# A fused attention and channel-mix kernel: weights loaded as f32, 64x64 tiles, x mixed from SBUF, and a second, general path

## The chip, the cores and the metric

The kernel runs on one core of one Trainium2 chip. The metric is the device time of one execution in microseconds; lower is better. The kernel before was timed three times: 218.06, 219.32 and 219.44, median 219.32. The profile is of one further execution, with a span of 216.9 us.

The core's engines are TensorE (PE; its weight loads are listed as PEld), VectorE (DVE), ScalarE (ACT), GpSimd (POOL) and SyncE (SP), which here only issues DMAs. Each works through its own queue in order.

## The reference

Two blocks one after the other. The first is a linear attention for 8 batches, 8 heads, 576 positions of 64 numbers each; the second is a channel mix over 512 channels (8 heads of 64), with a hidden width of 1024.

```python
q_s = softmax(q, over the 64 numbers);  k_s = softmax(k, over the 576 positions)
kv = k_s^T v                     # 64 x 64 for each head
x  = q_s kv                      # [8, 576, 512]
x_prev = x shifted by one position, zero at the first
xk = mu_k * x + (1 - mu_k) * x_prev
xr = mu_r * x + (1 - mu_r) * x_prev
k = max(xk @ w_k, 0);  v = (k * k) @ w_v
out = sigmoid(xr @ w_r) * v
```

Inputs and output are f32. The softmaxes subtract the maximum before the exponential in the reference. The kernel before leaves that out; for inputs of ordinary size the quotient is the same.

## The kernel before

Everything that TensorE multiplies is bf16, with f32 sums. A batch `b` goes through attention in two halves `u` of four heads each, and the half is laid out so that two heads stand side by side in 128 columns (`h`), and two such pairs on the two halves of the 128 partitions (`g`). 576 positions are split as 64 partitions times `J` = 9.

- `load` (L174): SP loads q, k and v as f32, a half at a time for batches 0 and 1, a whole batch at a time after that. `load_w` and `load_wv` (L240 to L252): GpSimd issues the loads of the three weight matrices, and the DMA turns them into bf16 on the way. `hold` (L189) makes some of these DMAs wait for a step of another engine, to give them an order.
- `exp` (L272, ACT) takes the exponentials of q and k; `cast_v` (L288, mostly GpSimd) makes v bf16, beside a column of ones; `sum_q` and `scale_q` (L292 to L306, DVE) normalize q.
- `turn_q` and `evict_q` (L308 to L320) transpose q on TensorE for batches 0 and 1; for the others `dma_turn_q` (L322) has a DMA do it.
- `kv` (L328): 18 matmuls with 64 rows, 128 columns of weights and 129 columns of data. Only the two diagonal 64x64 blocks of each result are used; column 128 is the sum of the exponentials. `norm_kv` (L342, DVE) divides and writes the blocks into a block-diagonal matrix whose other blocks were zeroed once.
- For batch 0 (`NM` = 1) `x_mixed` (L368) forms xk and xr directly on TensorE, from k'v matrices that were multiplied by mu and 1 - mu beforehand. For batches 1 to 7 `x` (L394) forms x in PSUM, the tile `xp`, with the first 64 columns holding the shifted start. `shift_x` (L405, ACT) reads `xp` and writes (1 - mu) times the previous position into `ak` or `ar`; `mix_x` (L411, DVE) reads the same `xp` and adds mu times x.
- `up` (L419, four matmuls of 288 columns for half of the positions), `relu` (L427, ACT) and `square` (L434, DVE) form k squared for one 128-wide slice `f` of the hidden width. `gate` and `tanh` (L442 to L452) and `down` and `finish` (L454 to L465) handle 128 rows `m` of a pair of batches; `store` (L467) writes them out in two DMAs. The sigmoid is formed as 1 + tanh of half the argument, with the factor 1/2 in relu.

PSUM has eight banks: `mm`, four single ones for up, gate, down and the early transposes and k'v, and `att`, two of two banks for k'v, x and mixed x.

The order of the work is made by a planner, the class `Plan` (L19). Each step has an engine, or several to choose from, a cost in us, a due time, steps it must follow, and slots of buffers that it needs. `run` (L46) plays the plan through: each free engine takes the ready step with the earliest due time whose slots are free. `emit` (L112) then writes the instructions out in that order, so each engine's queue holds them in that order. While nothing else is ready for TensorE before the first `up`, the plan puts in `warm` matmuls (L264), whose result is not used. The due times come from `sequence` and `spread` (L494 to L524): ups of batch `b` are interleaved with the gates and downs of the batches before and with the attention of batch `b` + 1.

Of the kernel before, what the change touches and what calls it, by code (L numbers as in the profile page):

```python
# [10 lines left out]
ALU = mybir.AluOpType  # L12
# [3 lines left out]
BF16 = mybir.dt.bfloat16  # L16


class Plan:  # L19
# [3 lines left out]

    def __init__(self, slots):
        self.slots, self.steps = dict(slots), []

    def slot(self, kind):
        return {"kind": kind, "users": 0, "taken": False}
# [9 lines left out]
    def link(self, s, after, uses):  # L38
# [7 lines left out]
    def run(self, fill=None):  # L46


        todo = {id(s): len(s["next"]) for s in self.steps}
        prev = {id(s): [] for s in self.steps}  # L50
        for s in self.steps:
            for n in s["next"]:
                prev[id(n)].append(s)
        back = [s for s in self.steps if not s["next"]]
        for s in back:
            for p in prev[id(s)]:
                p["due"] = min(p["due"], s["due"] - max(p["eng"].values()) - p["lat"])
                todo[id(p)] -= 1
                if not todo[id(p)]:
                    back.append(p)  # L60
        busy = {e: 0.0 for e in ("DVE", "ACT", "PE", "POOL", "DMA")}
        ready = [s for s in self.steps if not s["left"]]
        events, t, order = [], 0.0, []
        while True:
            for e in busy:
                if busy[e] > t + 1e-9:
                    continue
                for s in sorted(ready, key=lambda s: (s["due"], s["n"])):
# [3 lines left out]
                    for u in s["uses"]:  # L72
                        if not u["taken"]:
                            want[u["kind"]] = want.get(u["kind"], 0) + 1
                    if any(self.slots[k] < c for k, c in want.items()):
                        continue
                    for u in s["uses"]:
                        if not u["taken"]:
                            u["taken"] = True
                            self.slots[u["kind"]] -= 1  # L80
                    ready.remove(s)
                    break
                else:
                    if (not fill or e != fill[0] or "start" in fill[4]
                            or t < fill[3].get("start", 1e9) + 1.3):
                        continue
                    s = {"eng": {e: fill[1]}, "fn": fill[2], "lat": 0.0, "n": -1, "uses": [],
                         "next": [], "due": 0.0}
# [8 lines left out]
            while events and events[0][0] <= t + 1e-9:  # L97
# [6 lines left out]
                if what:  # L104
                    for u in s["uses"]:
                        u["users"] -= 1
                        if not u["users"]:
                            self.slots[u["kind"]] += 1
# [3 lines left out]
    def emit(self, fill=None):  # L112
        for s in self.run(fill):
# [5 lines left out]
def kernel(  # L119
# [21 lines left out]
    HS = S // 2  # L141

    const = ctx.enter_context(tc.tile_pool(name="const", bufs=1))
    ld = ctx.enter_context(tc.tile_pool(name="ld", bufs=2))
    att = ctx.enter_context(tc.tile_pool(name="att", bufs=2))
    grp = ctx.enter_context(tc.tile_pool(name="grp", bufs=2))
    mp = ctx.enter_context(tc.tile_pool(name="mp", bufs=3))
    op = ctx.enter_context(tc.tile_pool(name="op", bufs=4))
    psum = ctx.enter_context(tc.tile_pool(name="psum", bufs=1, space=bass.MemoryType.PSUM))
    MMB, ATB = 4, 2  # L150
    NM = 1


    ident = const.tile([128, 128], BF16, name="ident")
    identf = const.tile([16, 16], F32, name="identf")
    mus = const.tile([16, 64], F32, name="mus")
    mus2 = const.tile([16, 128], F32, name="mus2")
    half = const.tile([16, 2, 64], F32, name="half")
    mine = const.tile([16, 8], F32, name="mine")
    kvms = [const.tile([128, 2, 4, 128], BF16, name=f"kvm{i}") for i in range(2)]  # L160
# [5 lines left out]
    vbs = [const.tile([128, J, 130], BF16, name=f"vb{i}") for i in range(3)]  # L166
    kvbds = [const.tile([128, 2, 128], BF16, name=f"kvbd{i}") for i in range(2)]
    aks = [const.tile([128, S], BF16, name=f"ak{i}") for i in range(3)]
    ars = [const.tile([128, S], BF16, name=f"ar{i}") for i in range(3)]

    st: dict = {}


    def load(n, b, u, behind=None):  # L174


        src = {"q": q, "k": k, "v": v}[n]
        if u in (0, None):
            st[n, b] = ld.tile([128, 2, 2, J * D], F32, tag=n, name=f"{n}t")
        nu = 2 if u is None else 1  # L180
        d = nc.sync.dma_start(
            out=(st[n, b][:].rearrange("p u h f -> p (u h) f") if u is None
                 else st[n, b][:, u, :, :]),
            in_=bass.AP(tensor=src.tensor, offset=src.offset + (b * H + 4 * (u or 0)) * S * D,
                        ap=[[J * D, 128], [2 * S * D, 2 * nu], [1, J * D]]))
        if behind is not None:
            hold(d, behind)

    def hold(d, behind):  # L189

        tc.add_manual_dep(d.ins, st[behind].ins.name, mybir.DependencyInfo(
            mybir.DependencyClass.Sync, mybir.DependencyReason.DATA), reason="load order")

    def load_mu():
        for i, src in enumerate((moe_mu_k, moe_mu_r)):
            nc.scalar.dma_start(out=mus[8 * i:8 * i + 8, :],
                                in_=bass.AP(tensor=src.tensor, offset=src.offset,
                                            ap=[[64, 8], [1, 64]]))

    def pick():  # L200

        heads = identf[:].rearrange("p (a h g) -> p a h g", h=2, g=2)
        halves = const.tile([16, 2], F32, name="halves")
        nc.vector.reduce_sum(out=halves[:], in_=heads.rearrange("p a h g -> p h a g"), axis=AX.XY)
        nc.vector.tensor_copy(out=half[:], in_=halves[:, :, None].to_broadcast((16, 2, 64)))
        nc.vector.tensor_tensor(out=mine[:].rearrange("p (a g) -> p a g", g=2),
                                in0=heads[:, :, 0, :], in1=heads[:, :, 1, :], op=ALU.add)

    def mask_mu():

        nc.vector.tensor_copy(out=mus2[:].rearrange("p (h e) -> p h e", h=2),
                              in_=mus[:, None, :].to_broadcast((16, 2, 64)))
        st["musb"] = musb = mp.tile([16, 8, 64], F32, tag="th", bufs=5, name="musb")
        nc.vector.tensor_tensor(out=musb[:], in0=mus[:, None, :].to_broadcast((16, 8, 64)),
                                in1=mine[:, :, None].to_broadcast((16, 8, 64)), op=ALU.mult)

    def spread_mu():

        rows = psum.tile([128, 8, 64], F32, tag="mm", bufs=MMB, name="mur")
        nc.tensor.matmul(rows[:], lhsT=half[:].rearrange("p h e -> p (h e)"), rhs=st["musb"][:],  # L220
                         start=True, stop=True)
        cols = psum.tile([128, 512], F32, tag="mm", bufs=MMB, name="muc")
        nc.tensor.matmul(cols[:, 0:16], lhsT=mus2[:], rhs=identf[:], start=True, stop=True)
        st["mur"], st["muc"] = rows, cols

    def keep_mu():

        st["mub"] = mub = grp.tile([128, 4, CT, 64], F32, tag="k2", name="mub")
        minus = dict(scalar1=-1.0, scalar2=1.0, op0=ALU.mult, op1=ALU.add)
# [487 lines left out]
```

## Time and profile before

| | |
|---|---|
| median of three runs | 219.32 us |
| span of the profiled execution | 216.9 us |
| first `up` of batch 0 starts | 23.69 us |
| first `up` of batch 1 starts | 48.54 us |
| last matmul ends, about | 211.2 us |
| bytes read from HBM | 33.56 MB |

A row of the page's list of groups reads: line, engine, operation, output and inputs by the program's names, shapes, count, then busy us and mean ns of one, then the idle time of that engine before such instructions and who ended most of it:

```profile
L422 PE MATMUL up<-xk,wk_bf 128*128 128x288 bf16 x512 | 72.5, 286 | 5.0 <-ACT rel L431 4.3
L413 DVE SCALAR_TENSOR_TENSOR xk<-xp,mu,ak 128x576 bf16<-128x576 f32 x28 | 22.6, 814 | 7.4 <-ACT ak L408 4.8
```

Matmuls are pipelined: one row lasts 286 ns, but four of them in a stream take 0.49 us. A row of the timeline has the start in us, the duration in us (of several merged instructions together, with their count), engine, line and operation, and in brackets the idle time before it and who ended it. A row of the list of waits has who waited for whom, then the total in us, how often, and the longest. The chain of waits follows the work that ended last back to the start, and gives each piece the time until the next piece could go.

### The profile page before, as it was taken

Reading aid. Unit: us, or ns where it says so; the run is one execution under the profiler, and the core shown is the slowest. Engines: PE = TensorE matmul, PEld = TensorE weight load, DVE = VectorE, ACT = ScalarE, POOL = GpSimd, SP = SyncE. Lnnn points to the kernel's source line nnn. Section 1 sums busy time; section 2 is a strip of 40 time slices with the busy share of each in tenths; the row PEclk is TensorE's granted clock in tenths of the full one; section 3 lists DMA queues with packets and bytes.
Section 4 is the critical chain, followed back from the end, with each engine's and each line's share of the span. In section 5 each row is a group of like instructions: output and inputs, shape, how many; then the busy total and the mean of one; then the engine's idle time right before and its main releaser. Section 6 shows DMA issues by size and latency. Waiting matters only on the chain.

```text
span 216.9 us, 3766 instructions
## 1 busy us (share of the span) xinstructions
PE 195.5 (90%) x1407; PEld 113.7 (52%) x1428; DVE 159.7 (74%) x251; ACT 143.7 (66%) x265; POOL 26.4 (12%) x41
## 2 busy tenths in 40 slices
PE   0998989999988999999889996999799999999990
PEld 0454657447734665565445554565455565656440
DVE  4859996799999989988878597879887555324221
ACT  4455886997989679769586767669676667445020
POOL 2402820040050120050040002200000000000000
PEclk9999999999999999999999999999999999999997
DMA  6999999867999989998999796062406222322333
GB/s 224 381 241 368 345 189 362 335 182 211 210 353 311 302 282 313 271 352 276 304 229 365 175 383 128 14 141 48 103 3 151 48 51 48 88 57 51 72 85 87
DMA packets 34977, 44.15 MB, mean 204 GB/s; under 512 B 16016, under 2 KB 17552, under 8 KB 34960
## 3 DMA queue, kind: packets, MB, share of 16 engines
q1 hardware_dynamic: 32656, 41.16, 64.7%
q0 software_dynamic: 2192, 2.62, 7.1%
q8 instruction: 11, 0.18, 0.3%
q10 hardware_dynamic: 112, 0.14, 0.2%
q14 instruction: 6, 0.05, 0.1%
HBM read 33.56 MB, written 9.44 MB: 198 GB/s over the span
## 4 chain that ended last, share of the span: by engine, by line
PE 71%; DVE 16%; ACT 6%; issue 3%; DMA 1%; ACTq 0%; DVEq 0%
PE vp L457 27%; PE up L422 22%; PE rp L445 11%; PE kvp L338 4%; DVE qs L303 3%; ACT ar L408 3%; DVE xk L413 3%; PE warm L269 3%; DVE xr L413 2%; DVE rs L295 2%; PE xp L399 2%; DMA mus<-in_moe_mu_r_dram 1%; ACT rel L431 1%; PE qtp L313 1%; ACT ak L408 1%
## 5 line engine op out<-in xcount | busy, mean ns | idle before, releaser
L422 PE MATMUL up<-xk,wk_bf 128*128 128x288 bf16 x512 | 72.5, 286 | 5.0 <-ACT rel L431 4.3
L457 PE MATMUL vp<-wv_bf,k 128*128 128x512 bf16 x276 | 66.1, 379 | 0.7
L431 ACT ACTIVATE rel<-up 128x288 bf16<-128x288 f32 x128 | 49.8, 420 | 18.0 <-PE up L422 15.9
L422 PEld LDWEIGHTS <-wk_bf 128*128 128x128 bf16 x512 | 48.1, 98 | 23.8 <-issue 6.5
L457 PEld LDWEIGHTS <-k 128*128 128x128 bf16 x288 | 27.6, 98 | 30.6 <-issue 0.8
L463 DVE SCALAR_TENSOR_TENSOR ot<-th,vp 128x512 f32<-128x512 f32 x36 | 24.4, 685 | 24.2 <-PE vp L457 12.3
L445 PE MATMUL rp<-wr_bf,xr 128*128 128x512 bf16 x137 | 35.4, 379 | 1.7 <-ACT rel L431 1.3
L451 ACT ACTIVATE th<-rp 128x512 f32<-128x512 f32 x36 | 21.2, 613 | 18.4 <-PE rp L445 17.9
L286 POOL CAST vb<-vt 128x1152 bf16<-128x1152 f32 x15 | 19.4, 1311 | 102.4 <-DMA vt<-in_v_dram 87.0
L413 DVE SCALAR_TENSOR_TENSOR xk<-xp,mu,ak 128x576 bf16<-128x576 f32 x28 | 22.6, 814 | 7.4 <-ACT ak L408 4.8
L413 DVE SCALAR_TENSOR_TENSOR xr<-xp,mu,ar 128x576 bf16<-128x576 f32 x28 | 22.6, 812 | 7.0 <-ACT ar L408 6.5
L408 ACT ACTIVATE ar<-xp,om 128x575 bf16<-128x575 f32 x28 | 20.7, 746 | 9.8 <-DVE xk L413 9.8
L439 DVE TENSOR_TENSOR k<-rel 128x1152 bf16<-128x1152 bf16 x32 | 24.1, 754 | 2.8 <-ACT rel L431 2.5
L408 ACT ACTIVATE ak<-xp,om 128x575 bf16<-128x575 f32 x28 | 20.6, 746 | 8.3 <-PE xp L401 8.3
L303 DVE TENSOR_TENSOR qs<-eq,rr 128x1152 bf16<-128x1152 bf16 x16 | 24.6, 1538 | 0.2
L295 DVE TENSOR_REDUCE rs<-eq 128x18 f32<-128x1152 bf16 x16 | 21.6, 1349 | 1.0 <-ACT eq L274 0.7
L445 PEld LDWEIGHTS <-xr 128*128 128x128 bf16 x144 | 13.9, 98 | 15.0 <-issue 2.5
L274 ACT ACTIVATE eq<-qt 128x1152 bf16<-128x1152 f32 x16 | 19.0, 1186 | 1.5 <-DMA qt<-in_q_dram 1.5
L274 ACT ACTIVATE ek<-kt 128x1152 bf16<-128x1152 f32 x16 | 19.0, 1192 | 0.9 <-DMA kt<-in_k_dram 0.9
L338 PE MATMUL kvp<-vb,ek 64*128 64x129 bf16 x288 | 11.4, 218 | 0.0
L338 PEld LDWEIGHTS <-ek 64*128 64x128 bf16 x288 | 8.5, 94 | 4.6 <-issue 3.6
L399 PE MATMUL xp<-qT,kvbd 128*128 128x448 bf16 x28 | 9.3, 353 | 0.7 <-DVE xr L413 0.5
(54 smaller groups left out, 93.8 us busy)
## 6 DMA issues: line engine op xcount, KB each, us to landing
out_dram<-ot SPq DMA_DIRECT2D x71, 128.0 KB, 2.5
qt<-in_q_dram SPq DMA_DIRECT2D x6, 1152.0 KB, 6.8
kt<-in_k_dram SPq DMA_DIRECT2D x6, 1152.0 KB, 8.0
vt<-in_v_dram SPq DMA_DIRECT2D x6, 1152.0 KB, 8.1
qt<-in_q_dram SPq DMA_DIRECT2D x4, 576.0 KB, 7.1
kt<-in_k_dram SPq DMA_DIRECT2D x4, 576.0 KB, 7.3
vt<-in_v_dram SPq DMA_DIRECT2D x4, 576.0 KB, 10.6
wk_bf<-in_moe_w_k_dram POOLq DMA_DIRECT2D x4, 256.0 KB, 8.6
```

What stands on the lines that cost most here:

```text
L274: st["exp", n, b, u] = nc.scalar.activation(out=e[:].rearrange("p j (h d) -> p h j d", h=2), in_=st[n, b][:, u, :, :].rearrange("p h (j d) ...
L295: nc.vector.reduce_sum(out=rs[:], in_=eq, axis=AX.X)
L303: ew(eng).tensor_tensor(out=qs[:].rearrange("p j (h d) -> p (j h) d", h=2), in0=eq, in1=st["rr", b, u][:, :, None].to_broadcast((128, 2 * ...
L338: nc.tensor.matmul(ps[g][:, 0:129], lhsT=ek[r, j, :], rhs=vb[r, j, 0:129], start=(j == 0), stop=(j == J - 1))
L408: nc.scalar.activation(out=(aks, ars)[w][(4 * b + ct) % 3][:, 1:], in_=st["xp", b, u, g][:, 1:S], func=ACT.Copy, scale=om[:, c:c + 1])
L413: nc.vector.scalar_tensor_tensor(out=blend(b, ct, w), in0=st["xp", b, u, g][:, 64:], scalar=mu[:, 4 * w + ct:4 * w + ct + 1], in1=(aks, ar ...
L422: nc.tensor.matmul(ps[:, 0:HS], lhsT=wk_bf[:, ct, 128 * f:128 * f + 128], rhs=st["xk", b][:, ct, HS * h:HS * h + HS], start=(ct == 0), sto ...
L431: nc.scalar.activation(out=st["rel", b, f // 2][:, f % 2, HS * h:HS * h + HS], in_=st["up", b, f, h][:, 0:HS], func=ACT.Relu, scale=0.5 ** ...
L439: nc.vector.tensor_tensor(out=st["k2", b // 2][:, 2 * f2:2 * f2 + 2, o:o + S], in0=r[:], in1=r[:], op=ALU.mult)
L445: nc.tensor.matmul(ps[:], lhsT=st["xr", i][:, ct, 128 * m:128 * m + 128], rhs=wr_bf[:, ct, :], start=(ct == 0), stop=(ct == CT - 1))
L457: nc.tensor.matmul(ps[:], lhsT=st["k2", i][:, f, 128 * m:128 * m + 128], rhs=wv_bf[:, f, :], start=(f == 0), stop=(f == FT - 1))
L463: nc.vector.scalar_tensor_tensor(out=ot[:], in0=st["th", i, m][:], scalar=1.0, in1=st["vp", i, m][:], op0=ALU.add, op1=ALU.mult)
```

## The change

The same function is computed, from the same inputs, on the same engines. What differs:

- **Loads.** All loads stand in one SP queue, in the order q, q, k, v, k, v of batch 0; w_k in two pieces; w_r; batch 1; w_v in two pieces, which wait until w_k's buffer has been cast. The weights arrive as f32 in the buffers that later hold `k2` and `xr`, and are cast to bf16 on chip in ten pieces, most of them on GpSimd. Loads of all batches are a half at a time, with three buffers each. `hold` is gone.
- **64x64 tiles.** `kv` multiplies each head by itself: 36 matmuls of 64 rows, 64 columns of weights and 65 columns of data. `x` uses eight matmuls of 64 rows and 64 columns. The block-diagonal matrices and their zeros go; `norm_kv` becomes one reciprocal and one multiplication.
- **x from SBUF.** `evict_x` copies x from PSUM to SBUF (`xs`) on ACT in two parts, `prefix` copies the shifted start on GpSimd, `shift_x` runs on GpSimd or ACT (the planner puts 31 on GpSimd and 17 on ACT), and `mix_x` reads `xs` in place of PSUM.
- **Two batches mixed by TensorE** (`NM` = 2): batches 0 and 1 take the way of `x_mixed`, on 64x64 tiles, with `weigh_kv` on DVE.
- **relu** takes 576 columns at once; `square` may run on ACT.
- **PSUM**: three tiles of two banks (`two`) for up, k'v, x and transposes, and two of one bank (`one`) for gate and down.
- **General path.** The reciprocals of all sums are kept in `inv`. Near the end `watch`, `gather` and `judge` count those within 1e-6 to 1e6; every engine reads the flag, and if one is outside, a second program (`general`) computes everything again with the maxima subtracted. It more than doubles the instructions of the program, and is skipped with these inputs.
- **Planner**: buffers are chosen by the plan, due times start at 16.5 for batch 0's ups and 34.0 for batch 1's, and `warm` matmuls go into the gaps of the finished plan: six stand in TensorE's queue. In that queue three downs of batch 0 stand ahead of the first `up` of batch 1.

The core of the diff:

```diff
-                d = nc.gpsimd.dma_start(
...
-    def load_wv():
-        nc.gpsimd.dma_start(out=wv_bf[:], in_=bass.AP(
-            tensor=moe_w_v.tensor, offset=moe_w_v.offset, ap=[[C, 128], [128 * C, FT], [1, C]]))
...
+    def load_wk(a):
+        nc.sync.dma_start(out=wk_raw()[:, a, :, :], in_=bass.AP(
+            tensor=moe_w_k.tensor, offset=moe_w_k.offset + a * F // 2,
+            ap=[[F, 128], [128 * F, CT], [1, F // 2]]))
...
+    def load_wv(a):
+        nc.sync.dma_start(out=wv_raw()[:, 4 * a:4 * a + 4, :], in_=bass.AP(
+            tensor=moe_w_v.tensor, offset=moe_w_v.offset + 4 * a * 128 * C,
+            ap=[[C, 128], [128 * C, 4], [1, C]]))
+
+    def cast_wk(eng, a, c):
+        copy(eng, wk_bf[:, :, 512 * a + 256 * c:512 * a + 256 * c + 256],
+             wk_raw()[:, a, :, 256 * c:256 * c + 256])
...
+        ps, ek, vb = at("two", "kv", b, u), at("ek", b, u), at("vb", b, u)
         for j in range(J):
             for g in range(2):
-                r = slice(64 * g, 64 * g + 64)
-                nc.tensor.matmul(ps[g][:, 0:129], lhsT=ek[r, j, :], rhs=vb[r, j, 0:129],
-                                 start=(j == 0), stop=(j == J - 1))
-        st["kvp", b, u] = ps if b < 2 else t
...
-        if b < 2:
+                for h in range(2):
+                    r = slice(64 * g, 64 * g + 64)
+                    nc.tensor.matmul(ps[64 * h:64 * h + 64, g, 0:65],
+                                     lhsT=ek[r, j, 64 * h:64 * h + 64], rhs=vb[r, j, h, :],
+                                     start=(j == 0), stop=(j == J - 1))
...
+        rz = inv_k(b, u)
+        nc.vector.reciprocal(out=rz, in_=ps[:, :, 64])
+        nc.vector.tensor_tensor(out=dst[:], in0=ps[:, :, 0:64],
+                                in1=rz[:, :, None].to_broadcast((128, 2, 64)), op=ALU.mult)
+
+    def weigh_kv(b, u, w):
+        nc.vector.tensor_tensor(
+            out=at("kvm", b, u)[:, w, :, :, :].rearrange("p o g e -> p o (g e)"),
+            in0=at("kvn", b, u)[:].rearrange("p g e -> p (g e)")[:, None, :].to_broadcast(
+                (128, 2, 128)),
+            in1=mub(u)[:, w, :, :], op=ALU.mult)
...
+    def x(b, u, c):
+        ps, qT, kvs = at("two", "x", b, u, c), at("qT", b, u), at("kvs", b, u)
+        lo, n = PARTS[c]
+        for g in range(2):
+            for h in range(2):
+                r = slice(64 * h, 64 * h + 64)
+                nc.tensor.matmul(ps[64 * g:64 * g + 64, h, 0:64 * n], lhsT=kvs[r, g, :],
+                                 rhs=qT[r, lo:lo + n, 64 * g:64 * g + 64], start=True, stop=True)
...
+    def evict_x(b, u, c):
+        lo, n = PARTS[c]
+        copy("ACT", at("xs", b, u)[:, :, 64 + 64 * lo:64 + 64 * (lo + n)],
+             at("two", "x", b, u, c)[:, :, 0:64 * n])
+
+    def prefix(b, u):
+        xs = at("xs", b, u)
+        copy("POOL", xs[:, :, 1:64], xs[:, :, S:S + 63])
...
+    def shift_x(eng, b, u, h, w):
+        ct = 2 * u + h
+        o, i, s = at("aw", b, ct, w)[:], at("xs", b, u)[:, h, 0:S], om[:, 4 * w + ct:4 * w + ct + 1]
+        if eng == "ACT":
+            nc.scalar.activation(out=o, in_=i, func=ACT.Copy, scale=s)
         else:
-            nc.vector.reciprocal(out=rz[:], in_=ps[:, :, 128])
-        for h2 in range(2):
...
-    def mix_x(b, u, g, w):
-        ct = 2 * u + g
+            nc.gpsimd.tensor_scalar(out=o, in0=i, scalar1=s, scalar2=1.0, op0=ALU.mult,
+                                    op1=ALU.mult)
+
+    def mix_x(b, u, h, w):
+        ct = 2 * u + h
         nc.vector.scalar_tensor_tensor(
-            out=blend(b, ct, w), in0=st["xp", b, u, g][:, 64:],
-            scalar=mu[:, 4 * w + ct:4 * w + ct + 1],
-            in1=(aks, ars)[w][(4 * b + ct) % 3][:], op0=ALU.mult, op1=ALU.add)
-
-
-    def up(b, f, h):
-        ps = psum.tile([128, 512], F32, tag="mm", bufs=MMB, name="up")
+            out=blend(b, w)[:, ct, :], in0=at("xs", b, u)[:, h, 64:],
+            scalar=mu[:, 4 * w + ct:4 * w + ct + 1], in1=at("aw", b, ct, w)[:], op0=ALU.mult,
+            op1=ALU.add)
+
...
+    def up(b, f):
+        ps, xk = at("two", "up", b, f), at("xk", b)
+        for a in range(2):
+            for ct in range(CT):
+                nc.tensor.matmul(ps[:, a, 0:HS], lhsT=wk_bf[:, ct, 128 * f:128 * f + 128],
+                                 rhs=xk[:, ct, HS * a:HS * a + HS], start=(ct == 0),
+                                 stop=(ct == CT - 1))
...
+    def relu(b, f):
+        nc.scalar.activation(
+            out=at("rel", b, f // 2)[:, f % 2, :].rearrange("p (a c) -> p a c", a=2),
+            in_=at("two", "up", b, f)[:, :, 0:HS], func=ACT.Relu, scale=0.5 ** 0.5)
...
+    def square(eng, b, f2):
+        o, r = S * (b % 2), at("rel", b, f2)
+        dst = at("k2", b // 2)[:, 2 * f2:2 * f2 + 2, o:o + S]
+        if eng == "ACT":
+            nc.scalar.activation(out=dst, in_=r[:], func=ACT.Square)
+        else:
+            nc.vector.tensor_tensor(out=dst, in0=r[:], in1=r[:], op=ALU.mult)
...
-    pl = Plan({"mm": MMB, "att": ATB, "eq": 3, "ek": 3, "qs": 2, "qT": 3, "vb": 3, "xk": 2, "xr": 2,
-               "k2": 2, "th": 5, "rel": 3, "ot": 4, "a0": 3, "a1": 3, "bd0": 1, "bd1": 1, "ldq": 2, "ldk": 2, "ldv": 2})
...
+    def watch():
+        nc.vector.tensor_scalar(out=okay[:], in0=inv[:], scalar1=LOW, scalar2=None, op0=ALU.is_ge)
+        nc.vector.scalar_tensor_tensor(out=okay[:], in0=inv[:], scalar=HIGH, in1=okay[:],
+                                       op0=ALU.is_le, op1=ALU.mult)
+        nc.vector.reduce_sum(out=count[:], in_=okay[:], axis=AX.X)
+
+    def gather():
+        nc.tensor.matmul(at("two", "flag")[0:1, 0, 0:1], lhsT=count[:], rhs=ones[:], start=True,
+                         stop=True)
+
+    def judge():
+        nc.vector.tensor_scalar(out=flag[:], in0=at("two", "flag")[0:1, 0, 0:1],
+                                scalar1=128.0 * NR - 0.5, scalar2=None, op0=ALU.is_lt)
+
+    def read_flag():
+        st["bad"] = nc.values_load(flag[:], min_val=0, max_val=1,
+                                   skip_runtime_bounds_check_because="a comparison gives 0 or 1")
+        tc.mark_branch_hint_location("general")
...
+    queue = [ld("q", 0, 0), ld("q", 0, 1), ld("k", 0, 0), ld("v", 0, 0), ld("k", 0, 1),
+             ld("v", 0, 1)]
+    for a in range(2):
+        queue.append(dma(2.7, 0.0, lambda a=a: load_wk(a), uses=[sl("k2", "w")]))
...
+    for a in range(2):
+        queue.append(dma(2.7, 0.0, lambda a=a: load_wv(a), uses=[sl("k2", "w")],
+                         after=[ev["wk", i] for i in range(4)]))
...
     with tc.manual_schedule():
-        pl.emit(("PE", 0.3, warm, ev["mup"], ev["up", 0, 0, 0]))
+        pl.emit(("PE", 0.6, warm, ev["mup"], ev["up", 0, 0]))
+        slot = Turns()
+        with tc.If(st["bad"] != 0, preferred_fallthrough_block=False, label="general"):
+            general()
```

More of the change, by code (lines that the diff above doesn't have):

```diff
@@ L83, in run @@
                 else:
[L84 to L88, printed above, removed]
+                    continue
                 s["start"], s["on"], s["cost"] = t, e, s["eng"][e]
@@ L161 @@
+    mine = const.tile([8, 4], F32, name="mine")
+    halves = const.tile([8, 2], F32, name="halves")
     mu = const.tile([128, 8], F32, name="mu")
@@ L189, in hold @@
[L189 to L224, printed above, removed]
```

769 lines of the change are left out of this document (408 added, 361 removed).

## The prediction

> **What bounds the kernel now.** I read the busy totals and the chain of waits first, then the timeline of the first 50 us, then the list of who waited for whom, and last the rows of the operations that change.
>
> ```profile
> PE 195.5 (90%) x1407; PEld 113.7 (52%) x1428; DVE 159.7 (74%) x251; ACT 143.7 (66%) x265; POOL 26.4 (12%) x41
> ...
> PE 71%; DVE 16%; ACT 6%; issue 3%; DMA 1%; ACTq 0%; DVEq 0%
> ```
>
> TensorE is the bound, but not throughout. The timeline gives two marks: the first `up` of batch 0, and the first `up` of batch 1. The GpSimd row between them shows when the third batch of v had landed.
>
> ```profile
> 23.69 3.10 PE L422 MATMUL up<-xk,wk_bf 128*128 128x288 bf16 x24
> ...
> 44.38 2.24 POOL L286 CAST vb<-vt 128x1152 bf16<-128x1152 f32 x2 [14.58 <-DMA vt<-in_v_dram]
> ...
> 48.54 0.65 PE L422 MATMUL up<-xk,wk_bf 128*128 128x288 bf16 x4
> 49.13 0.70 PE L338 MATMUL kvp<-vb,ek 64*128 64x129 bf16 x18
> ```
>
> From the chain, an `up` of four matmuls takes 0.49, a gate 0.865, a down 1.73, a k'v 0.63. All ups, gates and downs are 128 x 0.49 + 36 x 0.865 + 36 x 1.73 = 156.1 us. At 48.4 batch 0's ups, four gates and four downs are done (7.8 + 3.5 + 6.9 = 18.2), so 137.9 is left, and 12 k'v and 12 x pairs (x: 0.27 for each g, so 0.54): 12 x 1.17 = 14.0. The last matmul ends at 211.2: 162.8 us for 151.9 of work. Of the 10.9 lost, these waits name 6.3:
>
> ```profile
> ACT ar L408 <- DVE xk L413: 9.8, 12, 1.4
> ...
> PE up L422 <- ACT rel L431: 4.3, 3, 1.4
> ...
> PE rp L445 <- ACT rel L431: 1.3, 5, 0.5
> PE up L422 <- ACT th L451: 0.7, 1, 0.7
> ```
>
> ACT stands still behind a `shift_x` that waits for DVE to finish with the same PSUM tile `xp`; relu queues behind it, its PSUM is not freed, PE stops. The other 4.6 is spread thin and stays in my sum. After the last matmul come tanh, finish, store and its landing, 211.2 to 216.9: 5.7 us.
>
> **The change, part by part.** Sums are against the span, 216.9; the median of the runs, 219.32, lies 2.4 above it, and I add that at the end.
>
> *Loads.* Three batches (3 x 3.54 MB) and the weights (5.24 MB as f32) were read by 44.4, the first 0.59 MB by 4.5: 15.3 MB in 39.9 us, 384 GB/s of reading. The new single queue reads batch 0, w_k, w_r, batch 1, w_v: 12.33 MB, so w_v ends at 4.5 + 11.74 / 0.384 = 35.1. On the way v of batch 0 is in at 12.2, the halves of w_k at 14.9 and 17.6, w_r at 20.4, v of batch 1 at 29.6. GpSimd casts the weights at the rate of L286 (1.15 for 1152, so 1.02 per piece of 1024); w_v's last pieces are ready at about 36.2.
>
> *First ups.* DVE now stands in order: reduce 1.35 and reciprocal 0.27, the mu rows (2.0, from about 8.0), again 1.6, two scalings of 1.36, then norms, weighings and copies of about 0.43 each; the first mixed x can start at about 16.5 and its copies end at 19. GpSimd casts w_k from 14.9 to 20 beside the weighings, which puts 1 us on them: first up at about 20 instead of 23.7. But what follows waits for w_v: in the new order on PE three downs of batch 0 stand ahead of batch 1's first up. So 36.2 + 3 x 1.73 + 1.4 for the mixed x between them = 42.8. There are few warming matmuls left (30 before); the early ones took 0.43 against 0.216 later, while the granted clock reads 1.00, so I add 0.7: batch 1 starts at 43.5, with 7.8 + 3.5 + 5.2 = 16.5 done. Before: 48.4 with 18.2. Gain 4.9 - 1.7 = 3.2, from -4 (the loads run at the 306 GB/s that the first eight slices count as moved: w_v at 42.9) to 6.
>
> *k'v and x on 64x64 tiles.* k'v goes from 18 matmuls of 129 columns to 36 of 65, each with its own weight load. No row has a 64-column tile. Below: 0.63 x 65/129 = 0.32. Above: L338's 35 ns a piece, 1.26, or without overlap of loads still more (a rival). Nearest is the 63-column piece of x, about 30 ns: 36 x 30 = 1.08 one after another, and 0.68 if row halves overlap as in L338 (129 columns serially are 56 ns, measured 35). I take 0.70. x: eight matmuls, 2304 columns, 0.98 serially, 0.61 with that overlap, 0.38 if column halves overlap too; I take 0.50 for 0.54. Twelve of each: 14.4 for 14.0, +0.4, from -6 to +8.
>
> *x mixed from SBUF.* Away go 48 `shift_x` reads of PSUM on ACT (0.746); in come 24 copies (0.64 and 0.59), and the shifts divide: 31 on GpSimd, 17 on ACT. relu goes from two of 0.41 to one of about 0.66; some squares move to ACT. Over the two batches from 109.1 to 157.3 ACT is busy 34.2 and DVE 38.7, 17.1 and 19.3 in a period of 24.1. The new ACT load is within 1 us of the old; DVE loses about 1.9 (mix 0.82 to about 0.75, one square or more of 0.75). The wait of ACT for DVE on `xp` is gone, so the 6.3 can go. What is late next is this:
>
> ```profile
> 24.20 1.20 POOL L286 CAST vb<-vt 128x1152 bf16<-128x1152 f32 x1
> ...
> 24.22 2.40 DVE L303 TENSOR_TENSOR qs<-eq,rr 128x1152 bf16<-128x1152 bf16 x1
> ...
> 72.28 1.36 DVE L303 TENSOR_TENSOR qs<-eq,rr 128x1152 bf16<-128x1152 bf16 x1
> ```
>
> A DVE operation with two SBUF inputs stood still while GpSimd worked: 2.40 for 1.36. Now mix_x has two SBUF inputs as well. Per batch GpSimd is busy 2 x 1.15 + 5.2 shifts x 0.65 (the cast's rate; a dearer one is possible, 1.2) + 2 x 0.25 = 6.2 of 22, DVE has about 12.6 such operations, and each meets it 28% of the time for 0.4: 1.4 us. DVE is at 17.4 + 1.4 = 18.8 of a period that PE alone makes 22: it holds, with bubbles. Two slots for gate and down, three for everything else, take slack away too. I leave 3.0 of the 6.3: gain 3.3, from 6.3 to a loss (rival one).
>
> *General path.* Not entered with these inputs. `watch`, `judge` and the 1x1 matmul run beside the last downs, when DVE is 20% busy: nothing. Every engine loads a register from SBUF before the last two or three tiles and ends with a branch over the other path. No row shows either; below nothing is excluded, as both only add. Nearest is a DMA's landing, 2.5: between 0 (hidden under the last store) and 4; I take 1.5.
>
> Sum: 216.9 - 3.2 + 0.4 - 3.3 + 1.5 = 212.3, and 2.4: **214.7 us**.
>
> **Rivals.**
> [...] If each of the 12.6 waits is a whole shift (0.65) and some a cast, 8 us, DVE needs 25.4 a batch and becomes the bound; it decides from waits of 6.7 (17.4 + 6.7 = 24.1). Six batches x 1.3 = 7.8: 219.3 - 3.2 + 1.5 + 0.4 + 7.8 = 225.8; half way, 223. For: the 2.40. Against: only three of 16 scalings show it (median 1.358).
> [...]
> *Two, slower: weight loads bound the small tiles.* A load row lasts 94 ns; if only the two row halves overlap, k'v is 18 x 94 = 1.7, +1.07 x 12 = 12.8: 227. For: 36 loads replace 18. Against: L338's 18 loads fit in 0.52.
> [...]
> *Three: the loads give nothing.* At 306 GB/s batch 1 starts at 51.3: 222; at 345, 218.
> *Four, faster: all bubbles go and the tiles overlap fourfold:* 214.7 - 3.0 - 3 = 208.5.
>
> **How the numbers follow.** Forecast (211 to 218.5) 0.42, of which 0.1 lies within 1% of 219.3 (about what can be told from no change); four 0.17; one 0.18; two 0.08; three 0.15, of which 0.06 within 1%. Faster 0.32 + 0.17 = 0.49, same 0.16, slower 0.35. The range leaves out two and the worst of one and three above, and the last of four below: 207 to 225.
>
> **What would show it.** Batch 1's first `up` at 43 to 44, w_v's casts just before; k'v near 0.7 in the chain; no wait of ACT for DVE on an x tile; DVE at 18 to 19 a batch, mix_x near 0.75 with some at 1.4; the last matmul near 205. It is wrong if mix_x averages over 1.1, if a k'v takes over 1.2, or if w_v lands after 39.

## The result, and the profile after

| | before | after |
|---|---|---|
| median of 12 runs each, us | 219.22 (218.06 to 220.12) | 217.52 (214.92 to 218.65) |
| ratio after/before | | 0.9898, 95% interval 0.9866 to 0.9929 |
| profiled execution: time, span, us | 219.32, 216.9 | 218.41, 217.0 |

The kernel became 1.0% faster (0.7 to 1.3%); 2.1% was forecast. The ratio leaves out the four of the twelve executions after that lie over 1.5% above the fastest, which is one reason why it is lower than that of the medians, and the profiled execution, 0.9 us above the median, is one of the four. Its span is no shorter than that of before; 1.7 us of it are lost to a low clock behind a stop of TensorE, read below.

The page's busy totals after:

```profile
PE 186.2 (86%) x1799; PEld 106.6 (49%) x1824; DVE 154.8 (71%) x216; ACT 145.8 (67%) x205; POOL 70.6 (33%) x81
```

TensorE is busy for 9.3 us less in the same span. Most of this is no saving: the `warm` matmuls, whose result is not used, fell from 9.5 to 2.9 us. From the first `up` of batch 1 to the last matmul TensorE is busy 153.6 us of 164.5, where it was 154.8 of 162.7. The PE timeline gives the marks: the first `up` of batch 0 at 19.55 (23.69 before), the first of batch 1 at 45.25 (48.54), and a k'v and an x of a later batch (a k'v row lasts 0.75 at 10.78 and 0.48 from 32.30 on, though the granted clock reads 1.00 from 0 to 40).

```profile
19.55 5.15 PE L448 MATMUL two<-xk,wk_bf 128*128 128x288 bf16 x40
...
45.25 1.14 PE L448 MATMUL two<-xk,wk_bf 128*128 128x288 bf16 x8
...
68.51 0.48 PE L364 MATMUL two<-vb,ek 64*64 64x65 bf16 x36
68.92 1.15 PE L448 MATMUL two<-xk,wk_bf 128*128 128x288 bf16 x8
...
72.71 0.44 PE L415 MATMUL two<-qT,kvs 64*64 64x256 bf16 x8
73.08 1.90 PE L477 MATMUL one<-wv_bf,k 128*128 128x512 bf16 x8
```

From its start to the start of the next row a k'v now takes 0.41 us (0.63 before) and an x 0.37 (0.54). TensorE's waits from 45.2 us on (who waited for whom: us in total, times, longest):

```profile
PE two L448 <- DVE xk L438: 4.7, 4, 2.2
PE one L477 <- DVE ot L482: 2.5, 2, 1.7
PE two L415 <- DVE kvs L373: 1.0, 2, 0.6
```

The old waits for relu are gone, and ups now wait for `mix_x` on VectorE, downs for `finish`. The groups of the new mixing (busy us, mean ns of one, idle before):

```profile
L438 DVE SCALAR_TENSOR_TENSOR xk<-xs,mu,aw 128x576 bf16<-128x576 f32 x24 | 28.6, 1229 | 6.9 <-POOL aw L433 6.8
...
L433 POOL TENSOR_SCALAR aw<-xs,om 128x576 bf16<-128x576 f32 x31 | 29.8, 977 | 5.0 <-POOL xs L221 4.8
...
L438 DVE SCALAR_TENSOR_TENSOR xr<-xs,mu,aw 128x576 bf16<-128x576 f32 x24 | 22.2, 955 | 0.0
```

A `mix_x` takes 1.09 us on the mean of its 48. The list by tiles has the shortest, the median and the longest of each (in ns, then first and last start in us):

```profile
L438 DVE SCALAR_TENSOR_TENSOR xk<-xs,mu,aw x24: 806/1293/1704, 52.3 to 178.6; 128x576 bf16<-128x576 f32 x24
L438 DVE SCALAR_TENSOR_TENSOR xr<-xs,mu,aw x24: 803/806/1704, 54.2 to 180.8; 128x576 bf16<-128x576 f32 x24
```

A mix with two SBUF inputs thus took 0.81 when nothing of GpSimd's stood beside it (two in a row 1.53 at 65.89, behind the end of a cast). Most mixes of `xr` did, and only four of them, each beside a cast of v, took 1.70. Of the mixes of `xk`, 22 of 24 were longer than 0.9, 16 of them about 1.29, beside a shift. The timeline in front of batch 2's ups shows how one instance comes about (start, us, engine, what, and the wait ahead of it):

```profile
57.99 1.61 POOL L221 CAST vb<-ldv 128x1152 bf16<-128x1152 f32 x1 [4.35 <-PE two L415]
...
58.51 2.30 DVE L334 TENSOR_TENSOR qs<-eq,inv 128x1152 bf16<-128x1152 bf16 x1
...
59.55 1.41 POOL L221 COPY xs<-xs 128x126 f32<-128x126 f32 x1
...
61.05 2.69 POOL L433 TENSOR_SCALAR aw<-xs,om 128x576 bf16<-128x576 f32 x3
...
61.84 2.51 DVE L438 SCALAR_TENSOR_TENSOR xk<-xs,mu,aw 128x576 bf16<-128x576 f32 x2 [1.03 <-POOL aw L433]
...
63.18 0.28 PE L448 MATMUL two<-xk,wk_bf 128*128 128x288 bf16 x1 [2.19 <-DVE xk L438]
64.40 0.90 PE L448 MATMUL two<-xk,wk_bf 128*128 128x288 bf16 x5 [0.94 <-DVE xk L438]
...
65.95 2.63 PE L477 MATMUL one<-wv_bf,k 128*128 128x512 bf16 x6 [0.22 <-issue]
```

GpSimd's cast of v (1.15 alone) stretches the VectorE scaling from 1.36 to 2.30, the scaling stretches the small prefix copy from 0.29 to 1.41, the shifts start late, and shifts and mixes stretch each other: two mixes in 2.51 us. TensorE stands for 3.1 us, and the six matmuls of a down behind it take 2.63 instead of some 1.4: the granted clock reads 0.73, 0.50 and 0.92 in the three stretches of 2 us from 64 to 70, so 1.7 us are lost.

At the end the last store is issued at 210.48 and the span ends at 217.0, 6.5 us later (4.2 before).

### The profile page after: what moved, and what is told of

Read it like the earlier page. It is cut to its first block, busy times and chain, and to the rows that moved or that the text cites. A ratio compares the mean times of both kernels' runs of the same rounds, so it can differ in the third digit from the quotient of the medians.

```text
span 217.0 us, 4567 instructions
## 1 busy us (share of the span) xinstructions
PE 186.2 (86%) x1799; PEld 106.6 (49%) x1824; DVE 154.8 (71%) x216; ACT 145.8 (67%) x205; POOL 70.6 (33%) x81
## 5 line engine op out<-in xcount | busy, mean ns | idle before, releaser
L448 PE MATMUL two<-xk,wk_bf 128*128 128x288 bf16 x512 | 72.4, 286 | 6.1 <-DVE xk L438 4.7
L477 PE MATMUL one<-wv_bf,k 128*128 128x512 bf16 x274 | 67.7, 385 | 4.3 <-DVE ot L482 3.3
L453 ACT ACTIVATE rel<-two 128x576 bf16<-128x576 f32 x64 | 41.3, 651 | 29.7 <-PE two L448 29.2
L482 DVE SCALAR_TENSOR_TENSOR ot<-th,one 128x512 f32<-128x512 f32 x36 | 24.5, 683 | 30.0 <-PE one L477 20.4
L467 PE MATMUL one<-wr_bf,xr 128*128 128x512 bf16 x133 | 34.8, 379 | 1.1 <-ACT th L472 0.6
L438 DVE SCALAR_TENSOR_TENSOR xk<-xs,mu,aw 128x576 bf16<-128x576 f32 x24 | 28.6, 1229 | 6.9 <-POOL aw L433 6.8
L221 POOL CAST vb<-ldv 128x1152 bf16<-128x1152 f32 (+1 forms) x18 | 24.0, 1340 | 26.8 <-DMA ldv<-in_v_dram 20.6
L433 POOL TENSOR_SCALAR aw<-xs,om 128x576 bf16<-128x576 f32 x31 | 29.8, 977 | 5.0 <-POOL xs L221 4.8
L334 DVE TENSOR_TENSOR qs<-eq,inv 128x1152 bf16<-128x1152 bf16 x16 | 22.6, 1415 | 0.1
L438 DVE SCALAR_TENSOR_TENSOR xr<-xs,mu,aw 128x576 bf16<-128x576 f32 x24 | 22.2, 955 | 0.0
```

The costliest lines, as they stand in the source:

```text
L221: return {"DVE": nc.vector, "POOL": nc.gpsimd}[eng].tensor_copy(out=out, in_=in_)
L334: nc.vector.tensor_tensor(out=at("qs", b, u)[:].rearrange("p j (h d) -> p (j h) d", h=2), in0=at("eq", b, u)[:].rearrange("p j (h d) -> p ...
L433: nc.gpsimd.tensor_scalar(out=o, in0=i, scalar1=s, scalar2=1.0, op0=ALU.mult, op1=ALU.mult)
L438: nc.vector.scalar_tensor_tensor(out=blend(b, w)[:, ct, :], in0=at("xs", b, u)[:, h, 64:], scalar=mu[:, 4 * w + ct:4 * w + ct + 1], in1=at ...
L448: nc.tensor.matmul(ps[:, a, 0:HS], lhsT=wk_bf[:, ct, 128 * f:128 * f + 128], rhs=xk[:, ct, HS * a:HS * a + HS], start=(ct == 0), stop=(ct ...
L453: nc.scalar.activation(out=at("rel", b, f // 2)[:, f % 2, :].rearrange("p (a c) -> p a c", a=2), in_=at("two", "up", b, f)[:, :, 0:HS], fu ...
```

## Experiments

Each kernel is the changed one with the edit shown. A difference to the changed kernel is one between medians; its own executions spread from 214.92 to 218.65, and taken from the ratios to before, the gains below come out up to 1.4 us smaller. Two theories of the stops: P, VectorE operations with two SBUF inputs and GpSimd operations stretch each other; W, the chain copy, prefix, shift, mix through GpSimd is long by itself.

### The general path left out

```diff
-    a = pl.step("DVE", 1.0, d - 6.0, watch, after=[nk, ...
-    ...
-    pl.step("PE", 0.1, d, read_flag, after=[a])
-        with tc.If(st["bad"] != 0, ...): general()
```

> Left out: watch, gather, judge, read_flag, the branch and the second path behind it; all that is computed for these inputs stays. Theory of the end (the branch costs what the span shows behind the last store: 6.5 us after its issue, before 4.2): the stretch from the end of the last matmul to the end of the span falls from 7.3 us to 5 to 5.7, the time by 1.6 to 2.3 us, to about 215.5. Theory that the end is only the landing of the last store: the stretch stays at 7, the time at 217 to 217.5.

214.78 us, ratio to before 0.9827 (0.9783 to 0.9871), 2.7 us less than the changed kernel. Head and last row of its timeline:

```profile
core 0 of [0], span 213.2 us
...
209.63 0.55 ACTq L490 DMA_DIRECT2D out_dram<-ot  x1
```

The span ends 3.6 us after the last store's issue instead of 6.5. The end is a cost of its own. How much time it is worth is less sure: 0.7 us more was gained than the 215.5 expected, and the interval of the ratio just touches the changed kernel's (0.9866 to 0.9929).

### The shifts on GpSimd left out, and the wait for them alone

```diff
+    still = const.tile([128, S], BF16, name="still")        # zeroed once
-            ... in1=at("aw", b, ct, w)[:], op0=ALU.mult,
+            ... in1=still[:], op0=ALU.mult,
-            nc.gpsimd.tensor_scalar(out=o, in0=i, scalar1=s, ...)    # only without the shifts
```

> Left out: the 31 shift_x on GpSimd (the 17 on ScalarE stay); every mix_x reads a bfloat16 tile that was zeroed once, so the token before is missing from the mix. The order of all other instructions is that of the changed kernel. Theory P (VectorE operations with two SBUF inputs and GpSimd operations stretch each other): mix_x falls from a mean of 1.09 us (48 of them) to 0.75 to 0.85, VectorE's busy time by 10 us or more, the 4.7 us of up waiting for mix_x to under 1, the time to 211 to 213. Theory W (not the stretching, but the longer chain copy, prefix, shift, mix in front of the ups): the same time, but mix_x stays near 1.0 because the stretching is not what made it long.

> All shift_x stay on GpSimd and ScalarE, but mix_x reads the zeroed tile: the wait of mix_x for its shift is gone and GpSimd is as busy as before; the token before is missing from the mix. Theory P: mix_x stays near 1.05 us on the mean, the time stays above that of the run without the shifts by 2 us or more (215 to 217). Theory W: as fast as the run without the shifts, within 0.7 us.

208.9 us (0.9565, 0.9525 to 0.9606) without the 31 shifts; 211.22 (0.9672, 0.963 to 0.9713) with the shifts there but nothing waiting for them. The groups, first without, then with the shifts:

```profile
L439 DVE SCALAR_TENSOR_TENSOR xk<-xs,mu,still 128x576 bf16<-128x576 f32 x24 | 21.8, 950 | 4.0 <-ACT xs L221 4.0
```

```profile
L435 POOL TENSOR_SCALAR aw<-xs,om 128x576 bf16<-128x576 f32 x31 | 35.8, 1169 | 5.3 <-ACT xs L221 4.2
...
L440 DVE SCALAR_TENSOR_TENSOR xk<-xs,mu,still 128x576 bf16<-128x576 f32 x24 | 25.9, 1119 | 4.0 <-ACT xs L221 4.0
```

VectorE's busy time falls by 12 us without the shifts (142.8) and by 2 with them unread (152.8). The shifts are worth 8.6 us in all. Neither theory had the second number: 2.3 us stay when nothing waits, more than W allows, and 6.3 go, more than P said. The length of the chain and the stretching are not told apart here: both edits change both.

### mix_x with one SBUF input, still waiting for its shift

```diff
-            ... in0=at("xs", b, u)[:, h, 64:],
+            ... in0=bufs["two"][2][:, 0, None, 448:512].to_broadcast((128, J, 64)),
```

> mix_x takes its first operand from a constant strip of 64 columns in PSUM, repeated nine times, instead of x in SBUF (so x at the token itself is missing from the mix); it still waits for its shift, on GpSimd or ScalarE, and has the same size. It has one SBUF input instead of two. A few matmuls wait for a mix_x that reads the same bank, which can only cost. Theory P (the stretching makes the chain long): mix_x falls to 0.82 us (what it took from PSUM before), the shifts on GpSimd to 0.9 or less, the waits of up for mix_x from 4.7 to under 2 us, time 209 to 212.5. Theory W (GpSimd's steps are long by themselves, whatever VectorE does): shifts stay at 0.98, the waits at 4 us or more, time 215 to 217.

217.57 us (0.9885, 0.9839 to 0.993): no change against the changed kernel, where theory P gave 209 to 212.5, and inconclusive. `mix_x` did fall to 0.81 and the shifts to 0.78, but ups now waited 5.9 us for mixes of `xr`, which only shared a bank with them. In the second form each of the three slots holds the strip, and a mix takes the one that TensorE wrote neither last nor longest ago:

```diff
+            in0=bufs["two"][st["seen"][1]][:, 0, None, 448:512].to_broadcast((128, J, 64)),
```

> As the earlier run with the constant PSUM strip as mix_x's first operand (x at the token itself is missing), but the strip is in each of the three two-bank slots and each mix_x takes the one that TensorE wrote neither last nor longest ago, so that TensorE should rarely have to wait for a mix_x that only shares its bank. Shifts and prefix stay on GpSimd and mix_x waits for them. Theory P (what VectorE and GpSimd do to each other's instructions makes the time): mix_x 0.82, shifts 0.8 or less, waits of up for mix_x under 3 us, time 211 to 214.5. Theory W (the chain through GpSimd costs this even without that): waits of up for mix_x 4 us or more, 216 to 217.5.

210.16 us (0.9597, 0.955 to 0.9644), 7.4 us less than the changed kernel. Its groups, the shortest, median and longest mixes, and TensorE's waits:

```profile
L441 POOL TENSOR_SCALAR aw<-xs,om 128x576 bf16<-128x576 f32 x31 | 24.7, 810 | 4.1 <-POOL xs L227 4.0
...
L446 DVE SCALAR_TENSOR_TENSOR xr<-two,mu,aw 128x576 bf16<-128x576 f32 x24 | 18.8, 810 | 1.7 <-ACT rel L463 1.0 <-PE two L372 0.4 <-POOL vb L227 0.2
L446 DVE SCALAR_TENSOR_TENSOR xk<-two,mu,aw 128x576 bf16<-128x576 f32 x24 | 18.7, 812 | 7.8 <-POOL aw L441 7.0 <-PE two L458 0.5 <-ACT rel L463 0.3
```

```profile
L446 DVE SCALAR_TENSOR_TENSOR xk<-two,mu,aw x24: 805/811/819, 52.1 to 169.8; 128x576 bf16<-128x576 f32 x24
L446 DVE SCALAR_TENSOR_TENSOR xr<-two,mu,aw x24: 804/809/818, 54.7 to 171.9; 128x576 bf16<-128x576 f32 x24
```

```profile
PE two L458 <- DVE xk L446: 1.9, 2, 1.4
```

GpSimd has all its work, every mix waits for its shift as before (7.0 us of VectorE waiting for `aw`), and only the second SBUF input of `mix_x` is gone. This is theory P, at 7.4 us (6.6 from the ratios), better than the range it gave. No mix is longer than 0.82 now, and that is no gain of reading PSUM as such, since an undisturbed one from SBUF took 0.81 too. In the profiled executions some 1.7 us of the gain is the low clock behind the stop: this one has none between its first `up` and its last matmul. Shifts fell with the mixes, from 0.98 to 0.81 on the mean. Why the two stretch each other is shown by no run.

### Shifts, and the prefix, on ScalarE

```diff
-                    p = pl.step({"POOL": 0.7, "ACT": 0.7}, 0, dx + 1.5 + 0.7 * h + 1.4 * w,
+                    p = pl.step({"ACT": 0.77}, 0.77, dx + 1.5 + 0.7 * h + 1.4 * w,
```

> All 48 shift_x on ScalarE, nothing else changed; the plan orders anew. Theory P: mix_x falls to 0.75 to 0.9 us, ScalarE takes on 31 x 0.77 = 24 us (busy about 165 to 170, unless squares go over to VectorE), waits of up for mix_x under 2 us, time 213 to 216. Theory W: a shift is shorter by only 0.2 us of a chain of four steps, and ScalarE is fuller: 217 to 220.

210.2 us (0.9587, 0.9521 to 0.9652), better than P's range. ScalarE is busy 156.3 us, not 165, because eight squares stay with it instead of 15, and mixes take 0.89 on the mean. So nearly all that the kernel with the strip in three slots showed is to be had with the whole computation. The prefix alone on ScalarE, with the 31 shifts left on GpSimd:

```diff
-        copy("POOL", xs[:, :, 1:64], xs[:, :, S:S + 63])
+        copy("ACT", xs[:, :, 1:64], xs[:, :, S:S + 63])
```

> Only prefix (12 copies of 126 columns, 0.3 us when nothing stands in the way) goes from GpSimd to ScalarE; the 31 shifts on GpSimd stay where they are. In the changed kernel's trace the prefix of batch 2 took 1.41 us, behind a cast of v on its own queue and beside a VectorE scaling of 2.30 us. If that one link is what opens the hole of 3.1 us at 61 to 64 us and the slow clock behind it (1.5 us): 214 to 215.5. If the shifts and mixes make it (four of the 5 us between x and the first up are theirs): within 1 us of the changed kernel, 216.5 to 218.

217.6 us (0.9892, 0.9852 to 0.9931): nothing gained. The prefix of batch 2 fell from 1.41 to 0.33, and the time went into the next link, three shifts in 4.37 us, beside a scaling and a square of VectorE:

```profile
59.64 4.37 POOL L433 TENSOR_SCALAR aw<-xs,om 128x576 bf16<-128x576 f32 x3
```

From 45.2 us on, ups waited 0.9 us for `mix_x` instead of 4.7, but downs waited 3.5 us for a tanh (none before) and 3.7 for `finish` (2.5 before): the waits of the ups alone do not say what the stretching costs.

With both on ScalarE:

> All shift_x and prefix on ScalarE; GpSimd only casts v (and, early, weights). Against the run with the shifts alone there (210.2): its prefixes still took 0.55 us on the mean, so where one of them is in a hole 1 us goes: 208.5 to 210. If ScalarE (75% busy there) becomes the bound, 210.5 to 212.

209.8 us (0.9563, 0.9523 to 0.9604), the same as with the shifts alone. A hole of 1.57 and 0.45 us in TensorE's work, at batch 2's first ups, stays.

### Batch 2 mixed by TensorE

```diff
-    NM = 2
+    NM = 3
```

> Batch 2 is mixed by TensorE as well (NM = 3), everything else as in the changed kernel. The hole of 3.1 us that TensorE has at 61 to 64 us, waiting for batch 2's mix_x, and the slow clock behind it (1 to 1.5 us) go; TensorE gets four x_mixed pairs (4 x 0.69) for two x (2 x 0.44), 1.9 us more, and nine transposes twice (1.1 more). Theory P or W alike: -4 + 3 = about -1, 216 to 217.5. If the hole only moves to batch 3: 218 to 220.

214.96 us (0.9817, 0.9765 to 0.9869), 2.6 less, where 216 to 217.5 was expected (the interval overlaps a little with the changed kernel's); TensorE is busy 191.9 instead of 186.2, and the hole at 61 us is gone. Together with shifts and prefix on ScalarE:

> As the run with shifts and prefix on ScalarE, with batch 2 mixed by TensorE too. In the changed kernel this was worth 2.6 us because it went round the hole of batch 2. If moving the shifts has closed that hole already, only TensorE's extra work is left (1.9 us of x_mixed, 1.1 of transposes): 2 to 3 us slower than without it, 211 to 213. If there is still a hole there, the same time within 1 us.

208.81 us (0.9529, 0.9487 to 0.9571), against 209.8 without: 1 us faster. A hole had been left, and for this case the same time within 1 us was expected; the 2 to 3 us slower belonged to the case without one. TensorE is busy 2.8 us longer, and its idle time shrinks by more.

### The end together with the rest

> All shift_x on ScalarE and no watch, branch and second path (as in the two runs that did one of these alone; for these inputs nothing is missing). If the end is a cost of its own, behind everything, the two gains add: 210.2 - 2.3 to 2.7 = 207.5 to 208. If the end's gain came from other instructions being placed differently, less than 1 us is left of it: 209.3 to 210.2.

> As the run with shifts and prefix on ScalarE, and no watch, branch and second path (nothing that these inputs need is missing): the end's 2.0 to 2.7 us less than that run, 206.5 to 208; if the hole in front of batch 2's ups is gone too, the mean granted clock is at 0.995 or above and the spans at 204 to 206.

> Shifts and prefix on ScalarE, batch 2 mixed by TensorE, no watch, branch and second path. 208.8 without the last; the end was worth 1.1 to 2.7 us in three pairs: 206.3 to 207.7.

208.56 (against 210.2), 208.73 (against 209.8) and 207.14 us (0.9444, 0.9428 to 0.9459; against 208.81): the end gives 1.6, 1.1 and 1.7 us here, less than the 2.7 of the first pair and less than two of the three expectations. From the last store's issue to the end of the span the middle pair (209.8 and 208.73) has 5.5 and 3.6 us, 1.9 less. In its two profiled executions the clock took part of this back: both have the same hole, and the ups behind it took 2.73 us in one, with the granted clock at 1.00, and 4.19 in the other, with 0.51 and 0.64 in the 2 us stretches from 64 and 66. First the run with the general path, then without:

```profile
61.79 0.28 PE L448 MATMUL two<-xk,wk_bf 128*128 128x288 bf16 x1 [1.57 <-DVE xk L438]
62.52 2.73 PE L448 MATMUL two<-xk,wk_bf 128*128 128x288 bf16 x21 [0.45 <-DVE xk L438]
```

```profile
62.22 0.28 PE L448 MATMUL two<-xk,wk_bf 128*128 128x288 bf16 x1 [1.56 <-DVE xk L438]
62.95 4.19 PE L448 MATMUL two<-xk,wk_bf 128*128 128x288 bf16 x21 [0.45 <-DVE xk L438]
```

The kernel of 207.14 us beats both; it has no path for inputs out of range, as the kernel before had none. With that path, 208.81 is the fastest measured.

### PSUM slots, the tiles, and the order of the loads

```diff
-    bufs["two"] = [... for i in range(3)]
-    bufs["one"] = [... for i in range(2)]
+    bufs["two"] = [... for i in range(2)]
+    bufs["one"] = [... for i in range(4)]
```

> PSUM split anew: two slots of two banks and four of one bank, instead of three and two. The stops of downs for finish (2.5 us of waits, and 0.13 us in each of the last tiles) go, at most 3.3 us. If the third slot of two banks is what keeps ups going while relu, copies and k'v hold theirs, more than this comes back as ups that wait for relu: 219 to 224. If two are enough, 214 to 216.

228.03 us (1.0376, 1.0311 to 1.0442), above the 219 to 224 expected. Downs no longer wait for `finish`, and ups wait 6.3 us for `mix_x` and 4.2 for `norm_kv` (for relu, as was expected, 1.4); the third slot of two banks is worth more than the stops of downs.

```diff
-        for j in range(J):
+        for j in [*range(J), *range(J)]:
```

> Every k'v product is computed twice over (the second time from zero again, so its result is the same): 36 more matmuls of 65 columns in each of 16. If 36 of them really cost 0.48 us with the clock up (0.75 in the first 40 us), 12 x 0.48 + 4 x 0.75 = 8.8 us more work for TensorE, 5 to 9 us more time after what falls into holes: 222.5 to 226.5. If the profile's modelled ends hide the weight loads and one takes 0.9 us or more, 15 us and more: over 231.

221.88 us (1.0112, 1.0083 to 1.0141), 4.4 us more, just under the expected range. A row of 72 reads:

```profile
48.31 0.78 PE L364 MATMUL two<-vb,ek 64*64 64x65 bf16 x72
```

36 more matmuls with their weight loads add 0.30 us (0.78 - 0.48), 8.3 ns each, and 16 times 0.30 is 4.8. The time agrees with this only loosely, because the profiled execution also had its clock at 0.50 for 10.2 us, against 3.4 in that of the changed kernel. The 0.9 us or more for 36, with a time over 231, is refuted: the modelled ends hide no such cost.

```diff
-    queue += [ld("q", 1, 0), ld("q", 1, 1), ld("k", 1, 0), ...]    # from ahead of w_v
+    queue += [ld("q", 1, 0), ld("q", 1, 1), ld("k", 1, 0), ...]    # to behind it
```

> w_v is loaded ahead of batch 1's q, k and v instead of behind them. If w_v's landing (36 us) is what holds the order on TensorE up (three downs stand ahead of batch 1's first up), the downs run by 30 us, and the 1.5 us of stops at 33 to 44 us go: 215.5 to 217. If batch 1's path from its loads to its first up is the limit, that path starts 5.5 us later (2.1 MB at 384 GB/s) and the time rises by 2 to 5 us: 219.5 to 222.5.

221.01 us (1.0057, 1.0036 to 1.0079), 3.5 more: batch 1's first `up` came at 49.9, and TensorE stood for 3.1 us at 31. Its clock then read 0.50 for 6.8 us, which is part of the loss. Batch 1's loads came some 5.5 us later by the reckoning above and its first `up` 4.7, so batch 1's path from its loads had about 1 us to spare at most in the changed kernel. Nor does TensorE wait for w_v there: its waits from 28 us to that `up` are 0.7 us for a cast of v, 0.7 for a `finish` and 0.2 without a releaser.

## Why the prediction was wrong, and where it was right

The sum of the prediction, made again with the marks of the profile after (last matmul's end 209.7):

| step | forecast | measured |
|---|---|---|
| start | -3.2 | -1.4: 45.25 for 48.4 (48.54 in its row), with 16.5 instead of 18.2 us done |
| k'v and x | +0.4 | -4.6: 12 x 0.78 = 9.4 for 14.0 |
| bubbles | -3.3 | +4.5: 164.4 us for 139.6 + 9.4 of work, 15.4 lost for 10.9 |
| end | +1.5 | +1.6: 209.7 to 217.0, 7.3 for 5.7 |
| span | 212.3 | 217.0 |

The last step, from the span to the time, was taken as 2.4 us and is 1.4 in the profiled execution.

**The failed step is the one on x mixed from SBUF.** "Each meets it 28% of the time for 0.4: 1.4 us" took GpSimd's and VectorE's instructions as falling on each other by chance. They do not: a mix starts when its shift is done, and that is when the next shift starts, so 22 of the 24 mixes of `xk` were stretched. A mix was 0.81 alone, two in a row took 2.51 us beside shifts, and the mean was 1.09, not 0.75; a shift took 0.98 on the mean, not 0.65. VectorE came to 40.5 us in two batches (109.1 to 157.3), 20.3 each instead of 18 to 19. The 6.3 us of waits behind the x tile did go, as forecast: no wait of ScalarE for VectorE on such a tile is left. But 7.4 us for the stretching, and for the low clock behind one stop of it, came in their place, shown by the run with `mix_x` reading PSUM in three slots. What the rest of the 15.4 us is, beyond the 4.6 that the prediction left as spread thin, stays open. "It holds, with bubbles" was right of VectorE as a whole, 20.3 of 24.1; the loss lies in the chain ahead of a batch's first ups and in downs that wait for a `finish` queued behind mixes (1.73 us at 126.5 in the PE timeline).

**Rival one, VectorE's waits beside GpSimd, had the stretching and its size, but not the way.** It priced 7.8 us for a VectorE that is the bound at 25.4 us a batch. VectorE was not, at 20.3 of 24.1; the stretching costs about as much without that, because it makes the chain longer that TensorE waits for. That 7.8 and 7.4 are so near is chance. The mean of 1.09 us was just short of the 1.1 that the prediction named as its refutation.

**The tiles were mis-sized the other way.** 0.70 and 0.50 were taken, between 0.32 and 1.26; measured 0.41 and 0.37, with 36 loads and matmuls in 0.30 us when repeated. That is near the lower bound (0.32), the fourfold overlap of rival four, and rival two (227) is refuted: 36 matmuls of 65 columns one after another would take about 1.0 us at the rate of the ups (0.49 us for 4 x 288 columns), and 0.41 or 0.30 is less than half of that, so by this estimate more than two went on at a time, each with its weight load (8.3 ns for both in the repeat, where rival two took 94 for a load). By its own terms the sum of rival four is a little off: 214.7 - 3.0 - 3 is 208.7. The error of 5.0 us in the tiles and the one of 7.8 in the bubbles have opposite signs. The forecast missed by no more than 2.8 us in the median because they largely cancel, and that is luck.

**Start.** The first `up` of batch 0 came at 19.55 (20 forecast), w_v's last cast ended at 38.2 (36.2), and the first of three downs began at 37.2, 1 us late. From there 8.0 us, not 7.3, to batch 1's first `up`: three downs of 1.7, both halves of the mixed x, and 0.75 us of waiting for a `finish`. The three downs were ahead as forecast; that w_v's landing set the time is not what the profile shows, as no matmul from 28 us on waited for it, and with w_v loaded first batch 1 started 4.7 us later. Rival three (no gain from the loads, batch 1 at 51.3) is out.

**End.** 1.5 was taken between 0 and 4; the profile gives 1.6, and leaving the path out gave 1.1 to 2.7. It is not hidden beneath the landing of the last store: from the store's issue to the end of the span it adds 1.5 to 2.9 us in the four pairs (6.5 against 3.6 in the first).

## What to carry to other kernels

When an operand moves from PSUM to SBUF to free an engine, look at which instructions will then run at the same moment as GpSimd's: a producer on GpSimd and its consumer on VectorE with two SBUF inputs met in 22 of 24 cases here, not by the share of busy time. Price such a pair by its stretched rows, and put the producer on ScalarE if it has room (here 7.3 us). Small matmuls should be priced between full overlap of the quarters and none, with one row of them measured before a sum rests on it.

## What was not expected of the hardware

- A matmul of 65 columns on a 64x64 tile took 8.3 ns, its own weight load included, when 36 were repeated (0.30 us more); before, one of 129 columns on 64 rows took 35 ns (0.63 us for 18).
- The stretching was mutual and passed on. Shifts took 0.98 beside mixes with two SBUF inputs and 0.81 beside mixes with one; mixes took 1.09 with 31 shifts on GpSimd and 0.89 with none there. A GpSimd copy of 0.29 us took 1.41 beside a VectorE scaling that had itself taken 2.30 instead of 1.36 beside a cast.
- The same hole of 2 us in TensorE's work left the clock at 1.00 in one run (shifts and prefix on ScalarE: 21 matmuls in 2.73 us) and lowered it in another (the same without the general path: 4.19 us; granted 0.51 and 0.64 in the 2 us stretches from 64 and 66). In the profiles kept here, the clock fell between the first `up` and the last matmul for 3.4 us at a time, in two cases (k'v twice, and w_v first) for 6.8; in the changed kernel it read 0.50 from 64.90 to 68.32. The rows below (stretch, length, PE busy with its matmuls, clock, DMA) are of the second run: 2.00 us without matmuls, then the low clock:

```profile
60.62:64.03 3.41, 1.41 (x11) 1.00 1.04 396
64.03:67.44 3.41, 3.41 (x42) 0.50 1.22 229
```

  What makes the clock fall behind a hole in one run and not in the other is shown by no run.
